# Attention and mixture of experts on one core: the first batch's loads, the last groups' banks and evictions, the count, and the order of the instructions

## Chip, core and metric

One core of one Trainium2 chip runs the whole program. The metric is the device time of one execution in microseconds (us). The core has a matrix engine, PE (its weight loads are listed as PEld), a vector engine, DVE, a scalar engine, ACT, a general one, POOL, and SP, which here only issues DMAs. Each has its own instruction stream and runs it in order; they wait for each other by semaphores.

## The reference

`x` has 4 batches of 11456 tokens with 128 channels; `inducing` has 32 rows.

```python
def mab(q, kv):
    s = scale * (q @ kv.transpose(0, 2, 1))
    s = s - s.max(-1, keepdims=True)
    a = np.exp(s)
    a /= a.sum(-1, keepdims=True) + 1e-09
    return a @ kv
h = mab(I, x)          # 32 rows for each batch, over all its tokens
y = mab(x, h)          # each token over the 32 rows
```

Each row of `y` then goes through the best of 8 experts: `logits = y @ w_gate`, `e = argmax`, weight `p` = the softmax's value there, output `p * (relu(y @ w1[e]) @ w2[e])` with 1024 hidden units. All of it is float32.

## The kernel before

**Tiling.** A batch is cut into 6 groups of 15 x 128 tokens. A group is loaded by column (`xt`, 960 KB: channels on the partitions, used for scores), and for the sums over tokens also by row (`xn`, 967.5 KB). For some groups (`TURNED`) the rows are not loaded: PE transposes the column tile (L315) and ACT or DVE copies it (L325, L327). There are 12 buffers for `xt`, 3 for `xn`, 3 for results (`ob`), 8 for the tokens' weights (`et`). Of the eight PSUM banks three are for scores (`fe`), one for logits (`lp`) and four for all else (`ps`). In the first batch the row tiles that are loaded go into the `ob` buffers, which nothing else uses yet.

**A batch's first half, `attend`.** Two groups at a time: scores with the inducing rows (L199, `it_s`), their peak (DVE L364), spread of the peak over the partitions (POOL L367, PE L376, DVE L382), exponent (ACT L386), 32x32 transposes (DVE L394), sums over the tokens (PE L403, collected by DVE in `hs`). After six groups `induced` forms `h`: L457 and L458 on PE, division and `hT` on DVE (L468 to L470), then the expert that fits the batch, whose weights are gathered by POOL (`w1r`, `w2r`, L510). From these PE makes a 32x128 matrix `h4` (L539, L569, L583), by which the tokens' weights give the result directly, and a bound (`thr`, L603) that says for which tokens this holds.

**A batch's second half, `tokens`.** Three groups at a time (a trio): scores with `hc` (L199), peak (DVE L646 to L650), weights (ACT L654, `et`), logits (PE L658, all three groups summed into the one `lp` bank). Then the gating of the trio on DVE and ACT (L668 to L708, factors in `c_all`). For each group: the factors are turned (DVE L715, `cb`), weights times factors (POOL L718), four expert matmuls into four `ps` banks (PE L722, K = 32 each), four evictions by ACT (L733) into `ob`, and a store issued by ACT (L736).

**At the end** the tokens not covered by the bound are counted (L786 to L795: three steps on DVE, a matmul on PE, a cast), every engine loads the count (`nleft`, L797) and branches on it (L798); if it is above zero, a slow loop treats the rest. With these inputs it is zero.

**What sets the order.** `Plan.add` takes for each step its engine, a cost, what it comes after, a rank, and the buffers or banks that it takes and gives back. `Plan.order` is a list scheduler: it places next the step that can start first by these costs, and of equal ones the one of lower rank. Loads are steps of an engine called DMA there, 2.5 us each. The kernel's instructions are written in the resulting order; the layer that records them then puts each engine's instructions in an order of its own, which may set instructions of one step apart or move them past each other. On SP's queue the loads keep the plan's order, and a load whose buffer is not free holds up those behind it.

Of the kernel before, what the change touches and what calls it, by code (L numbers as in the profile page):

```python
# [31 lines left out]
F32 = mybir.dt.float32  # L32
I32 = mybir.dt.int32
AF = mybir.ActivationFunctionType
ALU = mybir.AluOpType
# [4 lines left out]
P = 128  # L40
# [95 lines left out]
def attn_moe_kernel(ctx, tc, xT, xn, indT, wg, w1, w2, consts, out):  # L136
# [18 lines left out]
    nc.vector.memset(gz[:, 0:1], 1.0)  # L155
    hT_all = const.tile([P, B, P], F32, name="hT_all")
    c_all = const.tile([P, B, NBLK], F32, name="c_all")
    it_s = const.tile([P, M], F32, name="it_s")
    nc.vector.tensor_scalar_mul(it_s, it_sb, SCALE)

# [111 lines left out]
    def buf(op, i=0):  # L272
        k, n = op["got"][i]
        return T[k][n]
# [22 lines left out]
    def by_row(b, g, rank, load, w):  # L297


        s = S[b]  # L300
        if g not in TURNED.get(b, ()):

            def load_xn():
                w.xn = rows(buf(op))
                nc.sync.dma_start(w.xn, xn[b, :, g * GB : (g + 1) * GB, :])


            op = plan.add("DMA", 2.5, load_xn, rank=rank - 2.7, take=("ob" if b == 0 else "xn",), lag=2.0)
            return [op], (op, 0)
        turns, kept = {}, []  # L310

        def turn(k0, n):
            ps = buf(turns[k0])
            for k in range(n):
                nc.tensor.transpose(  # L315
                    ps[:, k * P : (k + 1) * P], s.xt[g][:, k0 + k].rearrange("p q t -> p (q t)"), ident
                )

        def keep(k0, n, eng):
            if k0 == 0:  # L320
                w.xn = rows(buf(turns[0], 1))
            src = buf(turns[k0])[:, : n * P].rearrange("p (k c) -> p k c", c=P)
            dst = w.xn[:, k0 : k0 + n, 0:P]
            if eng == "ACT":
                nc.scalar.copy(dst, src)  # L325
            else:
                nc.vector.tensor_copy(dst, src)  # L327
# [17 lines left out]
        return kept, (turns[0], 1)  # L345

    def pair1(b, g0, rank, begin):
# [5 lines left out]
        def load_xt(w, g):  # L353
            if begin and g == 0:
                begin()
            nc.sync.dma_start(buf(w.load), xT[b, g])
            s.xt[g] = buf(w.load)
# [90 lines left out]
    def induced(b, rank):  # L448
# [54 lines left out]
                out=w.ii, in0=w.r1, scalar=-128.0, in1=pcol, op0=ALU.mult, op1=ALU.add  # L503
            )

        def gather():
            w.w1r = pl.wraw.tile([P, F], F32, name="w1r")
            w.w2r = pl.wraw.tile([P, F], F32, name="w2r")
            for dst, src in ((w.w1r, w1), (w.w2r, w2)):
                nc.gpsimd.indirect_dma_start(  # L510
                    out=dst, out_offset=None, in_=src, in_offset=bass.IndirectOffsetOnAxis(ap=w.ii[:, :1], axis=0)
                )

        def gate_matrix():

# [110 lines left out]
        f4 = plan.add("PE", 0.9, mm_h4, [f3], r, ("ps",), ((i5, 0),), lag=0.1)  # L626
# [8 lines left out]
    def tokens(b, g0):  # L635
# [91 lines left out]
                    stop=True,  # L727
                )

        def evict(w, q):  # L730
            if q == 0:
                w.ob = buf(w.ev)[:, : NQ * GW].rearrange("p (q n) -> p q n", q=NQ)
            nc.scalar.copy(w.ob[:, q, :], buf(w.b9, q)[:, :GW])  # L733

        def store(w, g):
            nc.scalar.dma_start(out[b, g], w.ob.rearrange("p q n -> p (q n)"))  # L736

        last = None
        for u, w in enumerate(some):
# [17 lines left out]
        for u, w in enumerate(some):  # L757
            g = g0 + u
            r = NG * b + g
            w.b7 = plan.add("DVE", 0.68, lambda w=w, u=u: turn_factors(w, u), [g2], r, ("cb",))  # L760
            b8 = plan.add("POOL", 1.2, lambda w=w: weigh(w), [w.b7], r, give=((w.b7, 0),))
            w.b9 = plan.add(
                "PE", 1.1, lambda w=w: experts(w), [b8, s.h4_op], r, ("ps",) * 4, ((w.b4, 0),), lag=0.1
            )
            ev = []
            for q in range(NQ):
                take = () if ev else ("ob",)
                ev.append(
                    plan.add(
                        "ACT", 0.5, lambda w=w, q=q: evict(w, q), [w.b9] + ev[:1], r, take, ((w.b9, q),)  # L770
                    )
                )
            w.ev = ev[0]
            st = plan.add("ACT", 0.05, lambda w=w, g=g: store(w, g), ev, r)
            s.experts_op = w.b9
            plan.add("DMA", 2.8, lambda: None, [st], r - 3, give=((w.ev, 0),), lag=2.0)
# [9 lines left out]
    nc.vector.memset(c_all[64:128, :, NBLK - 1 : NBLK], 1.0)  # L786
    left = const.tile([P, B * NBLK], F32, name="left")
    nc.vector.tensor_single_scalar(left, c_all.rearrange("p b n -> p (b n)"), 0.0, op=ALU.is_gt)
    nc.vector.tensor_scalar(left, left, -1.0, 1.0, op0=ALU.mult, op1=ALU.add)
    cnt = const.tile([P, 1], F32, name="cnt")  # L790
    nc.vector.tensor_reduce(cnt, left, AX.X, ALU.add)
    psn = T["ps"][0]
    nc.tensor.matmul(psn[:, 0:1], lhsT=ones, rhs=cnt, start=True, stop=True)
    nleft = const.tile([P, 1], I32, name="nleft")
    nc.vector.tensor_copy(nleft, psn[:, 0:1])  # L795
    main.close()
    nl = nc.values_load(nleft[0:1, 0:1], min_val=0, max_val=P * B * NBLK)  # L797
    with tc.If(nl > 0):  # L798
# [191 lines left out]
```

## Time and profile before

| | |
|---|---|
| three runs | 231.03, 234.84 (median), 235.23 us |
| the profiled execution | 233.27 us, its span 231.5 us |
| PE, DVE, ACT, POOL busy | 188.5, 132.0, 104.7, 40.3 us |
| mean granted PE clock | 0.892 |
| DMA | 63.78 MB, 276 GB/s on average |

The span runs from the first to the last instruction of the one profiled execution; the rest of its time lies around it. In rows of instructions stand the start, the duration, the engine, the source line, the operation, the tile written and the tiles read, their shape, and how many instructions the row joins; in brackets the idle time before and what ended it. A fp32 matmul leaves two records. Rows of stages give the busy us and the number of records of PE, PEld, DVE, ACT and POOL, then the granted clock (1.00 is full), the share of the DMA engines' time and GB/s. Rows of waits give the total, how often, and the longest.

### The profile page before, as it was taken

The page shows a single profiled execution, that of the slowest core. Times are in us where ns is not written, and L with a number is a line of the kernel's source. Part 1 is how long each engine was busy: PE and PEld are TensorE (multiplying, and loading weights), DVE is VectorE, ACT ScalarE, POOL GpSimd, SP SyncE. Part 2 cuts the span into 40 slices and gives each one's busy share as a digit, 9 for nine tenths or more (in the row PEclk, how much of TensorE's full clock was granted, in tenths as well). Part 3 has the DMA queues.
Part 4 walks back from the last instruction along what each step waited for, and adds up shares of the span by engine and source line. Part 5 has one row for each costly group of instructions (what it writes and reads, how often), then busy time and mean ns, then how long its engine had stood idle before and what let it go on. Part 6 is the DMA issues. An engine that isn't in the chain of part 4 may idle for free.

```text
span 231.5 us, 4416 instructions
## 1 busy us (share of the span) xinstructions
PE 188.5 (81%) x1694; PEld 94.7 (41%) x1695; DVE 132.0 (57%) x400; ACT 104.7 (45%) x212; POOL 40.3 (17%) x58
## 2 busy tenths in 40 slices
PE   0897588898997799989999959999598959984840
PEld 0565364456665233544352236535122224422520
DVE  0275536674489266874894680848844998037300
ACT  2243204263350827385735841396236532845630
POOL 2000003000003500060045000410530062303200
PEclk9999889999999889999999997999959995578555
DMA  6999999995369847997999990034427524627591
GB/s 222 426 428 423 427 423 422 415 417 194 94 253 342 352 171 288 355 365 266 326 426 418 428 369 15 4 150 195 170 71 280 235 105 173 254 100 327 243 394 58
DMA packets 10252, 63.78 MB, mean 276 GB/s; under 512 B 1392, under 2 KB 1520, under 8 KB 10224
## 3 DMA queue, kind: packets, MB, share of 16 engines
q1 hardware_dynamic: 5328, 35.62, 39.2%
q10 hardware_dynamic: 3744, 23.62, 25.0%
q0 software_dynamic: 1152, 4.19, 4.8%
q8 instruction: 15, 0.25, 0.4%
q14 instruction: 13, 0.11, 0.1%
HBM read 39.83 MB, written 23.59 MB: 274 GB/s over the span
## 4 chain that ended last, share of the span: by engine, by line
PE 55%; DVE 19%; DMA 10%; ACT 6%; issue 3%; POOL 3%; SPq 0%; ACTq 0%; DVEq 0%; POOLq 0%
PE ps L722 16%; PE fe L199 15%; PE lp L658 8%; PE ps L403 8%; DMA xt<-in_xT 6%; PE ps L315 4%; DMA w1r<-in_w,ii 4%; ACT ob L733 3%; DVE cb L715 3%; POOL et L718 3%; DVE e L394 2%; DVE mx L364 2%; ACT e1t L386 2%; DVE mx L646 1%; ACT xn L325 1%
## 5 line engine op out<-in xcount | busy, mean ns | idle before, releaser
L733 ACT COPY ob<-ps 128x480 f32<-128x480 f32 x96 | 47.5, 573 | 34.0 <-PE ps L722 33.8
L722 PE MATMUL ps<-et,h 32*128 32x480 f32 x192 | 47.9, 739 | 10.3 <-POOL et L718 6.2
L718 POOL TENSOR_TENSOR et<-et,cb 128x480 f32<-128x480 f32 x24 | 28.4, 1211 | 56.2 <-DVE cb L715 36.8
L199 PE MATMUL fe<-xt,it_s 128*32 128x480 f32 x192 | 29.6, 609 | 9.7 <-DMA xt<-in_xT 9.7
L325 ACT COPY xn<-ps 128x512 f32<-128x512 f32 (+1 forms) x42 | 22.4, 570 | 26.1 <-PE ps L315 23.8
L364 DVE TENSOR_REDUCE mx<-fe 128x1 f32<-128x480 f32 x24 | 15.6, 652 | 27.9 <-PE fe L199 25.7
L722 PEld LDWEIGHTS ps<-et,h 32*128 32x128 f32 x192 | 17.6, 216 | 33.7 <-POOL et L718 13.8
L199 PE MATMUL fe<-xt,hc 128*32 128x480 f32 x192 | 29.4, 613 | 1.6 <-ACT e1t L386 1.1
L315 PE MATMUL ps<-csb,xt 128*128 128x128 f32 x180 | 27.1, 291 | 1.5 <-DMA xt<-in_xT 1.5
L658 PE MATMUL lp<-et,gzw 128*128 128x480 f32 x48 | 27.5, 661 | 0.5 <-ACT et L654 0.5
L654 ACT ACTIVATE et<-fe,rn 128x480 f32<-128x480 f32 x24 | 16.0, 671 | 26.1 <-DVE rn L650 16.6
L403 PE MATMUL ps<-xn,e 128*32 128x129 f32 x630 | 25.7, 282 | 1.7 <-DVE e L394 1.7
L315 PEld LDWEIGHTS ps<-csb,xt 128*128 128x128 f32 x180 | 21.7, 153 | 13.1 <-issue 6.2
L403 PEld LDWEIGHTS ps<-xn,e 128*32 128x32 f32 x630 | 21.8, 113 | 9.0 <-DVE e L394 2.5
L394 DVE STREAM_TRANSPOSE e<-e1t 128x480 f32<-128x480 f32 x24 | 15.1, 656 | 7.9 <-ACT e1t L386 7.8
L386 ACT ACTIVATE e1t<-fe,rn 128x480 f32<-128x480 f32 x24 | 14.8, 667 | 10.2 <-DVE rn L382 9.8
L646 DVE TENSOR_REDUCE mx<-fe 128x1 f32<-128x480 f32 x24 | 15.4, 643 | 6.1 <-PE fe L199 5.8
L715 DVE STREAM_TRANSPOSE cb<-c_all 128x480 f32<-128x480 f32 x24 | 15.4, 663 | 5.5 <-POOL et L718 5.0
L367 POOL TENSOR_TENSOR mq<-mx,csb 128x8 f32<-128x8 f32 x12 | 2.4, 201 | 91.3 <-DVE mx L364 91.2
L658 PEld LDWEIGHTS lp<-et,gzw 128*128 128x128 f32 x48 | 8.0, 207 | 13.5 <-issue 7.0
L668 DVE STREAM_TRANSPOSE lv<-lp 128x480 f32<-128x480 f32 x8 | 5.4, 671 | 14.3 <-PE lp L658 14.3
L199 PEld LDWEIGHTS fe<-xt,it_s 128*32 128x32 f32 x192 | 6.3, 113 | 16.0 <-issue 10.4
(94 smaller groups left out, 149.2 us busy)
## 6 DMA issues: line engine op xcount, KB each, us to landing
xt<-in_xT SPq DMA_DIRECT2D x24, 960.0 KB, 9.7
out<-ob ACTq DMA_DIRECT2D x24, 960.0 KB, 3.8
xn<-in_xn SPq DMA_DIRECT2D x9, 967.5 KB, 8.0
ob<-in_xn SPq DMA_DIRECT2D x3, 967.5 KB, 15.7
csb<-in_consts SPq DMA_DIRECT2D x1, 134.5 KB
w1r<-in_w,ii POOLq DMA_INDIRECT x4, 7.7
w2r<-in_w,ii POOLq DMA_INDIRECT x4, 9.3
it_sb<-in_indT ACTq DMA_DIRECT2D x1, 16.0 KB
```

The lines of the kernel that those rows point to most:

```text
L199: nc.tensor.matmul(blk(ps[32 * q : 32 * q + 32, :GW]), lhsT=lhsT, rhs=xt_g[:, :, q, :], start=True, stop=True)
L315: nc.tensor.transpose(ps[:, k * P : (k + 1) * P], s.xt[g][:, k0 + k].rearrange("p q t -> p (q t)"), ident)
L325: nc.scalar.copy(dst, src)
L364: nc.vector.tensor_reduce(s.mx[:, g : g + 1], w.ps[:, :GW], AX.X, ALU.max)
L386: nc.scalar.activation(w.et, w.ps[:, :GW], AF.Exp, bias=pr.rn)
L394: nc.vector.transpose(w.e1, w.et)
L403: nc.tensor.matmul(hp[32 * j : 32 * j + 32, :], lhsT=blk(w.e1)[:, k, :], rhs=w.xn[:, k, :], start=(n < 4), stop=(n >= 2 * GB - 4),)
L658: nc.tensor.matmul(buf(some[0].b5)[:, :GW], lhsT=s.gzw[:, u * P : (u + 1) * P], rhs=w.et, start=(u == 0), stop=(u == NW - 1),)
L715: nc.vector.transpose(blk(w.cb), c.unsqueeze(2).to_broadcast([P, GB, 32]))
L718: nc.gpsimd.tensor_tensor(out=w.et, in0=w.et, in1=w.cb, op=ALU.mult)
L722: nc.tensor.matmul(buf(w.b9, q)[:, :GW], lhsT=s.h4[32 * q : 32 * q + 32, :], rhs=w.et[32 * q : 32 * q + 32, :], start=True, stop=True,)
L733: nc.scalar.copy(w.ob[:, q, :], buf(w.b9, q)[:, :GW])
```

## The change

1. **First batch.** The column loads of batch 0 get rank r - 60 (before: r - 3), its row loads rank - 30 (before: rank - 2.7). So all six column tiles are loaded first, then the three row tiles.
2. **Last groups.** In the last trio of the last batch the middle group takes the three `fe` banks and the `lp` bank in place of the `ps` banks, and of each group's four banks DVE evicts the second and fourth. All stores of the last batch are issued by SP, in two halves of 480 KB each.
3. **Count.** It becomes three steps of the plan, after the factors of all groups; on PE it has a low rank. One DVE instruction is saved.
4. **Gather.** The two gathers become two steps of the plan with 1.1 and 1.0 us; the instructions are the same.
5. **Order.** After the plan's order has been written out, every instruction gets a dependence without a semaphore on the one before it on its engine, so the recording layer keeps the plan's order.

```diff
-            op = plan.add("DMA", 2.5, load_xn, rank=rank - 2.7, take=("ob" if b == 0 else "xn",), lag=2.0)
+            op = plan.add(
+                "DMA", 2.5, load_xn, rank=rank - 2.7 if b else rank - 30, take=("xn" if b else "ob",), lag=2.0
+            )
...
-            w.load = plan.add("DMA", 2.5, lambda w=w, g=g: load_xt(w, g), rank=r - 3, take=("xt",), lag=2.0)
+            w.load = plan.add(
+                "DMA", 2.5, lambda w=w, g=g: load_xt(w, g), rank=r - 3 if b else r - 60, take=("xt",), lag=2.0
+            )
...
-        i5 = plan.add("POOL", 2.0, gather, [i4], r, ("wraw",), lag=8.5)
+        i5 = plan.add("POOL", 1.1, lambda: gather("w1r", w1), [i4], r, ("wraw",), lag=7.9)
+        i6 = plan.add("POOL", 1.0, lambda: gather("w2r", w2), [i4], r + 0.001, lag=9.3)
...
-            nc.scalar.copy(w.ob[:, q, :], buf(w.b9, q)[:, :GW])
+            if eng == "ACT":
+                nc.scalar.copy(w.ob[:, q, :], buf(w.b9, q)[:, :GW])
+            else:
+                nc.vector.tensor_copy(w.ob[:, q, :], buf(w.b9, q)[:, :GW])
...
+            if b < B - 1:
+                nc.scalar.dma_start(out[b, g], w.ob.rearrange("p q n -> p (q n)"))
+            else:
+                h = NQ * GW // 2
+                nc.sync.dma_start(
+                    out[b, g][:, half * h : half * h + h], w.ob[:, 2 * half : 2 * half + 2].rearrange("p q n -> p (q n)")
+                )
...
+            end = b == B - 1 and g0 + NW == NG
+            banks = ("fe", "fe", "fe", "lp") if end and u == 1 else ("ps",) * 4
+            w.b9 = plan.add("PE", 1.1, lambda w=w: experts(w), [b8, s.h4_op], r, banks, ((w.b4, 0),), lag=0.1)
...
+                eng = "DVE" if end and q % 2 else "ACT"
...
+    co = plan.add("DVE", 1.2, count, [o for s in S for o in s.g2], NG * B)
+    mc = plan.add("PE", 0.5, mm_count, [co], NG * B - 9, ("ps",), lag=0.1)
+    plan.add("DVE", 0.2, copy_count, [mc], NG * B - 9, give=((mc, 0),))
+
     for op in plan.order():
         op["fn"]()
...
+    order = mybir.DependencyInfo(mybir.DependencyClass.NoSync, mybir.DependencyReason.DATA)
+    latest = {}
+    for ins in list(nc.cur_bb.bb.instructions):
+        if ins.engine in latest:
+            tc.add_manual_dep(ins, latest[ins.engine], order, reason="the plan's order")
+        latest[ins.engine] = ins.name
```

Where the instructions stand now is shown at three places. The numbers behind tile names are those of buffers; they are shifted between the two programs, since three tiles were added, and L numbers shift as well (L199 is now L202, L457 L465, L658 L666, L722 L730).

SP's queue at the start of the program, before (`xt_91` to `xt_96` are the column tiles of batch 0, `ob_106` to `ob_108` its row tiles, `xt_97` and `xn_103` the first group of batch 1):

```order
L356 DMA xt_91<-in_xT 128x1920
L356 DMA xt_92<-in_xT 128x1920
L356 DMA xt_93<-in_xT 128x1920
L356 DMA xt_94<-in_xT 128x1920
L305 DMA ob_106<-in_xn 128x1935
L356 DMA xt_95<-in_xT 128x1920
L305 DMA ob_107<-in_xn 128x1935
L356 DMA xt_96<-in_xT 128x1920
L305 DMA ob_108<-in_xn 128x1935
L356 DMA xt_97<-in_xT 128x1920
```

And now (`xt_94` to `xt_99`, `ob_109` to `ob_111`, `xt_100`):

```order
L361 DMA xt_94<-in_xT 128x1920
L361 DMA xt_95<-in_xT 128x1920
L361 DMA xt_96<-in_xT 128x1920
L361 DMA xt_97<-in_xT 128x1920
L361 DMA xt_98<-in_xT 128x1920
L361 DMA xt_99<-in_xT 128x1920
L308 DMA ob_109<-in_xn 128x1935
L308 DMA ob_110<-in_xn 128x1935
L308 DMA ob_111<-in_xn 128x1935
L361 DMA xt_100<-in_xT 128x1920
```

The column tiles of groups 4 and 5 have moved from places 6 and 8 to places 5 and 6; the last row tile stays at place 9.

PE where the last batch's `h` is formed, before (`et_119` and `et_120` are groups 0 and 1 of the batch before):

```order
L457 MATMUL ps_132<-csb,hs 128x128
L458 MATMUL ps_132<-csb,hs 128x32
L658 MATMUL lp_130<-et_115,gzw_135 128x480
L199 MATMUL fe_128<-xt_96,hc 32x480 x4
L722 MATMUL ps_134<-et_119,h_1446 128x480
L481 MATMUL ps_131<-wg_sb,hT_all 128x8
L722 MATMUL ps_133<-et_119,h_1446 128x480
L482 MATMUL ps_131<-wg_sb,hb 128x8
L722 MATMUL ps_132<-et_119,h_1446 128x480
L199 MATMUL fe_127<-xt_97,hc 32x480 x4
L199 MATMUL fe_129<-xt_98,hc 32x480 x4
L722 MATMUL ps_131<-et_119,h_1446 128x480
```

And now (`et_122` is that group 0; `xt_100` and `xt_101` are groups 0 and 1 of the last batch):

```order
L465 MATMUL ps_136<-csb,hs 128x128
L466 MATMUL ps_136<-csb,hs 128x32
L489 MATMUL ps_137<-wg_sb,hT_all 128x8
L490 MATMUL ps_137<-wg_sb,hb 128x8
L202 MATMUL fe_131<-xt_100,hc 32x480 x4
L202 MATMUL fe_132<-xt_101,hc 32x480 x4
L730 MATMUL ps_135<-et_122,h_1367 128x480
L730 MATMUL ps_134<-et_122,h_1367 128x480
L730 MATMUL ps_136<-et_122,h_1367 128x480
L730 MATMUL ps_137<-et_122,h_1367 128x480
```

The four matmuls of a group's experts stand together now, behind the small matmuls of `h` and the first scores of the last batch, and no longer with other work between them.

PE at the last logits, before (`et_116` is the last group of the third batch, `et_117` to `et_122` are groups 0 to 5 of the last one):

```order
L722 MATMUL ps_131<-et_116,h_1446 128x480
L658 MATMUL lp_130<-et_120,gzw_136 128x480
L722 MATMUL ps_134<-et_117,h_1872 128x480
L722 MATMUL ps_133<-et_117,h_1872 128x480
L722 MATMUL ps_132<-et_117,h_1872 128x480
L722 MATMUL ps_131<-et_117,h_1872 128x480
L658 MATMUL lp_130<-et_121,gzw_136 128x480
L658 MATMUL lp_130<-et_122,gzw_136 128x480
L722 MATMUL ps_134<-et_118,h_1872 128x480
L722 MATMUL ps_133<-et_118,h_1872 128x480
```

And now (`et_118` and `et_119` are groups 4 and 5 of the third batch, `et_120` to `et_125` the last batch):

```order
L666 MATMUL lp_133<-et_124,gzw_139 128x480
L730 MATMUL ps_135<-et_118,h_1367 128x480
L730 MATMUL ps_134<-et_118,h_1367 128x480
L730 MATMUL ps_136<-et_118,h_1367 128x480
L730 MATMUL ps_137<-et_118,h_1367 128x480
L666 MATMUL lp_133<-et_125,gzw_139 128x480
L730 MATMUL ps_135<-et_119,h_1367 128x480
L730 MATMUL ps_134<-et_119,h_1367 128x480
L730 MATMUL ps_136<-et_119,h_1367 128x480
L730 MATMUL ps_137<-et_119,h_1367 128x480
```

The last group's logits now come ahead of the third batch's last experts; before they came behind the experts of the last batch's first group. After these rows PE has the experts of the last batch in the order 0, 1, 4 (in `fe` and `lp`), the count's matmul, 2, 3, 5.

More of the change, by code (lines that the diff above doesn't have):

```diff
@@ L157, in attn_moe_kernel @@
     c_all = const.tile([P, B, NBLK], F32, name="c_all")
+    left = const.tile([P, B * NBLK], F32, name="left")
+    cnt = const.tile([P, 1], F32, name="cnt")
+    nleft = const.tile([P, 1], I32, name="nleft")
     it_s = const.tile([P, M], F32, name="it_s")
@@ L504, in pick, with gather @@
             )
[L506 to L512, printed above, removed]
+        def gather(n, src):
+            t = pl.wraw.tile([P, F], F32, name=n)
+            setattr(w, n, t)
+            nc.gpsimd.indirect_dma_start(
+                out=t, out_offset=None, in_=src, in_offset=bass.IndirectOffsetOnAxis(ap=w.ii[:, :1], axis=0)
+            )
         def gate_matrix():
@@ L625, in induced @@
         f3 = plan.add("DVE", 0.9, mask_g, [f2], r)
-        f4 = plan.add("PE", 0.9, mm_h4, [f3], r, ("ps",), ((i5, 0),), lag=0.1)
+        f4 = plan.add("PE", 0.9, mm_h4, [f3, i6], r, ("ps",), ((i5, 0),), lag=0.1)
         f4a = plan.add("ACT", 0.3, copy_h1, [f4], r, give=((f4, 0),))
@@ L728, in experts, with evict, store @@
                 )
-        def evict(w, q):
+        def evict(w, q, eng):
             if q == 0:
                 w.ob = buf(w.ev)[:, : NQ * GW].rearrange("p (q n) -> p q n", q=NQ)
-            nc.scalar.copy(w.ob[:, q, :], buf(w.b9, q)[:, :GW])
-        def store(w, g):
-            nc.scalar.dma_start(out[b, g], w.ob.rearrange("p q n -> p (q n)"))
+            if eng == "ACT":
+                nc.scalar.copy(w.ob[:, q, :], buf(w.b9, q)[:, :GW])
+            else:
+                nc.vector.tensor_copy(w.ob[:, q, :], buf(w.b9, q)[:, :GW])
+        def store(w, g, half):
+            if b < B - 1:
[4 more added lines that the diff above has]
+                    out[b, g][:, half * h : half * h + h], w.ob[:, 2 * half : 2 * half + 2].rearrange("p q n -> p (q n)")
+                )
         last = None
@@ L761, in tokens @@
             b8 = plan.add("POOL", 1.2, lambda w=w: weigh(w), [w.b7], r, give=((w.b7, 0),))
-            w.b9 = plan.add(
-                "PE", 1.1, lambda w=w: experts(w), [b8, s.h4_op], r, ("ps",) * 4, ((w.b4, 0),), lag=0.1
-            )
+            end = b == B - 1 and g0 + NW == NG
+            banks = ("fe", "fe", "fe", "lp") if end and u == 1 else ("ps",) * 4
+            w.b9 = plan.add("PE", 1.1, lambda w=w: experts(w), [b8, s.h4_op], r, banks, ((w.b4, 0),), lag=0.1)
             ev = []
@@ L767, in tokens @@
                 take = () if ev else ("ob",)
+                eng = "DVE" if end and q % 2 else "ACT"
                 ev.append(
                     plan.add(
-                        "ACT", 0.5, lambda w=w, q=q: evict(w, q), [w.b9] + ev[:1], r, take, ((w.b9, q),)
+                        eng,
+                        0.5 if eng == "ACT" else 0.65,
+                        lambda w=w, q=q, e=eng: evict(w, q, e),
+                        [w.b9] + ev[:1],
+                        r,
+                        take,
+                        ((w.b9, q),),
                     )
@@ L773, in tokens, with count, mm_count, copy_count @@
             w.ev = ev[0]
-            st = plan.add("ACT", 0.05, lambda w=w, g=g: store(w, g), ev, r)
             s.experts_op = w.b9
-            plan.add("DMA", 2.8, lambda: None, [st], r - 3, give=((w.ev, 0),), lag=2.0)
+            if b < B - 1:
+                st = [plan.add("ACT", 0.05, lambda w=w, g=g: store(w, g, 0), ev, r)]
+            else:
+                st = [
+                    plan.add("SP", 0.05, lambda w=w, g=g, h=h: store(w, g, h), [ev[0]] + ev[2 * h : 2 * h + 2], r)
+                    for h in range(2)
+                ]
+            plan.add("DMA", 2.8, lambda: None, st, r - 3, give=((w.ev, 0),), lag=2.0)
+        s.g2 = g2, w.b7
+    def count():
+        nc.vector.memset(c_all[64:128, :, NBLK - 1 : NBLK], 1.0)
+        nc.vector.tensor_scalar(
+            left, c_all.rearrange("p b n -> p (b n)"), 0.0, 1.0, op0=ALU.is_gt, op1=ALU.is_lt
+        )
+        nc.vector.tensor_reduce(cnt, left, AX.X, ALU.add)
+    def mm_count():
+        nc.tensor.matmul(buf(mc)[:, 0:1], lhsT=ones, rhs=cnt, start=True, stop=True)
+    def copy_count():
+        nc.vector.tensor_copy(nleft, buf(mc)[:, 0:1])
     for b in range(B):
@@ L781, in attn_moe_kernel @@
             tokens(b, g)
+    co = plan.add("DVE", 1.2, count, [o for s in S for o in s.g2], NG * B)
+    mc = plan.add("PE", 0.5, mm_count, [co], NG * B - 9, ("ps",), lag=0.1)
+    plan.add("DVE", 0.2, copy_count, [mc], NG * B - 9, give=((mc, 0),))
     for op in plan.order():
         op["fn"]()
[L786 to L795, printed above, removed]
+    order = mybir.DependencyInfo(mybir.DependencyClass.NoSync, mybir.DependencyReason.DATA)
[4 more added lines that the diff above has]
+        latest[ins.engine] = ins.name
     main.close()
```

## The prediction

> **What bounds the kernel now.** I read busy time, granted clock (PEclk, 1.00 is full) and DMA share by stage. I cut the span where PE forms the `h` of a batch (L457), because a batch's tokens cannot begin before its `h`.
>
> ```profile
> span 231.5 us, 4416 instructions
> core 0: us, PE busy (x) PEld busy (x) DVE busy (x) ACT busy (x) POOL busy (x), PEclk, DMA share, GB/s
> 0.00:32.40 32.40, 21.84 (x288) 14.96 (x289) 13.08 (x29) 8.62 (x16) 1.92 (x14) 0.95 0.95 389
> 32.40:62.80 30.40, 25.92 (x345) 16.48 (x343) 18.32 (x55) 11.36 (x24) 2.76 (x6) 1.00 0.80 316
> 62.80:113.00 50.20, 46.08 (x444) 22.47 (x445) 33.24 (x105) 27.20 (x56) 9.88 (x13) 0.97 0.80 299
> 113.00:161.00 48.00, 43.10 (x416) 21.27 (x417) 31.42 (x100) 26.64 (x55) 9.50 (x11) 0.96 0.65 263
> 161.00:223.00 62.00, 51.23 (x206) 19.23 (x205) 35.78 (x113) 30.86 (x64) 16.25 (x14) 0.75 0.50 202
> ```
>
> Up to 32.4 us the DMAs are full (0.95) and PE is not. In the middle PE leads, at 85 to 92% of each stage, at full clock. The last stage is the odd one: half the matmul records of the stages before it (206 against 444 and 416) and yet the longest, 62 us, at a clock of 0.75; ACT and DVE are busy for only about half of it. So it is bound by waits in turn. The table of waits for 161 us to the end names them:
>
> ```profile
> POOL et L718 <- DVE cb L715: 32.3, 3, 13.3
> ACT ob L733 <- PE ps L722: 23.2, 11, 3.9
> DVE lv L668 <- PE lp L658: 11.7, 2, 9.1
> ```
>
> In turn: PE brings the logits late to DVE, DVE the factors late to POOL, POOL the weights late to PE, PE the results late to ACT. The prices are therefore looked for at the two ends, the first `h` and the stage after the last one.
>
> **Start.** A load of 960 KB moves at some 428 GB/s here, thus one every 2.3 us.
>
> ```profile
> xt<-in_xT SPq DMA_DIRECT2D x24, 960.0 KB, 9.7
> 10.00:15.00 5.00, 5.00 (x41) 3.11 (x39) 3.36 (x7) 2.49 (x5) 0.20 (x1) 1.00 1.02 430
> 6.45 1.83 PE L199 MATMUL fe<-xt,it_s 128*32 128x480 f32 x8 [6.45 <-DMA xt<-in_xT]
> 25.20 0.67 DVE mx L364
> 28.34 3.20 PE L403 MATMUL ps<-ob,e 128*32 128x129 f32 x58 [1.74 <-DVE e L394]
> 32.38 0.49 PE L457 MATMUL ps<-csb,hs 128*128 128x128 f32 x2
> ```
>
> The first group is there at 6.45. The column load of group 5 was the eighth of the queue, so 6.45 + 7 x 2.3 = 22.6; its peak is taken at 25.2, its sums start 3.1 us later and end at 31.5, and `h` follows at 32.4. Now it is the sixth: 18.0. The last row load stays ninth, 6.45 + 8 x 2.3 = 24.9, and with the column chain out of the way this becomes the bound: 24.9, about 2 us for the sums of groups 4 and 5, then the scores of the next batch's first group, which stand ahead of `h` in PE's order and whose load is tenth (27.2 + 0.9): `h` at 28.3, **4.1 us** earlier. The bytes are the same and batch 1's loads land as before, so batch 1 can give some of it back: bounds 0 and -4.1. I take -3, since the second stage is bound by DMA only for its first half (share 0.80) and PE then has batch 0's tokens earlier.
>
> **Order.** In the old order three groups of experts are split: other matmuls stand between their four banks. In the new one all 24 stand whole.
>
> ```profile
> 92.13 1.07 PE L722 MATMUL ps<-et,h 32*128 32x480 f32 x2
> 206.29 1.09 PE L722 MATMUL ps<-et,h 32*128 32x480 f32 x8
> 165.84 1.07 PE L722 MATMUL ps<-et,h 32*128 32x480 f32 x2 [2.53 <-POOL et L718]
> 167.16 1.47 PE L722 MATMUL ps<-et,h 32*128 32x480 f32 x2
> 169.09 1.96 PE L722 MATMUL ps<-et,h 32*128 32x480 f32 x2
> 166.94 0.56 ACT L733 COPY ob<-ps 128x480 f32<-128x480 f32 x1 [3.93 <-PE ps L722]
> 175.51 0.56 ACT L733 COPY ob<-ps 128x480 f32<-128x480 f32 x1 [3.87 <-PE ps L722]
> 176.54 1.95 ACT L733 COPY ob<-ps 128x480 f32<-128x480 f32 x4
> ```
>
> One bank alone (two records) takes 1.07, four together 1.09. The split group near 90 us (three pieces) thus costs 2 x 1.07 = 2.1 us of PE: **-2** (0 to -2.1). The one at 166 us is dear: its four evictions last from 166.94 to 176.07, 9.1 us where a whole group takes 1.95, and the next groups queue behind them for the same banks. 7.2 us at most; **-5**, since DVE and POOL go on meanwhile and the order of `h` differs (0 to -7.2).
>
> By the last `h` the new order has done two logits and one score group more than the old. That work moves from the last stage ahead of it: nothing in the sum.
>
> The last logits are the next place:
>
> ```profile
> 203.78 2.58 PE L658 MATMUL lp<-et,gzw 128*128 128x480 f32 x4
> 206.40 0.68 DVE L668 STREAM_TRANSPOSE lv<-lp 128x480 f32<-128x480 f32 x1 [9.11 <-PE lp L658]
> 212.19 3.61 POOL L718 TENSOR_TENSOR et<-et,cb 128x480 f32<-128x480 f32 x3 [13.30 <-DVE cb L715]
> 216.15 5.93 PE L722 MATMUL ps<-et,h 32*128 32x480 f32 x16 [0.72 <-ACT ob L733]
> 218.11 0.56 ACT L733 COPY ob<-ps 128x480 f32<-128x480 f32 x1 [0.73 <-PE ps L722]
> 220.79 0.56 ACT L733 COPY ob<-ps 128x480 f32<-128x480 f32 x1 [0.73 <-PE ps L722]
> ```
>
> They are done at 206.4, and 5.8 us of gating lie between them and the first weighting. Now they stand two expert groups earlier, ahead of the third batch's last one. Such a group takes 1.95 us where ACT sets the pace and 2.7 at this clock (evictions of two groups begin at 218.11 and 220.79, each after 0.73 idle). Two make 3.9 to 5.4: **-4** (0, if ACT is still behind, to -5.4).
>
> **Last groups and end.** The last three took from the first weighting, 212.19, to the last eviction, 220.79 + 1.95 = 222.74: 10.5 us. DVE's copy of a PSUM bank is bounded by its 128x512 row, 0.69 against ACT's 0.56, so two banks on each cost 1.4 us a group instead of 1.95. But in PE's order the last batch now ends 0, 1, 4, count, 2, 3, 5. Group 4 has banks of its own; it also has to wait for its weighting, second of the last three, and group 2, long ready, stands behind it, with four evictions on ACT. From the first weighting: 2 x 1.2 until group 4 is weighted, 1.1 and 1.1 for groups 4 and 2 on PE, 1.95 to evict group 2, 0.7 for the first bank of group 3, 3 x 1.4 to evict 3, 4 and 5: 11.5 us at full clock, +1; some 2 us more at half clock. I take **+1.5** (-2, if group 2 comes through in time, to +3).
>
> ```profile
> out<-ob ACTq DMA_DIRECT2D x24, 960.0 KB, 3.8
> 10.21 0.69 DVE L327 COPY xn<-ps 128x512 f32<-128x512 f32 x1 [1.22 <-PE ps L315]
> 222.79 0.58 PE L793 MATMUL ps<-cnt,ones 128*128 128x1 f32 x2 [0.71 <-ACT ob L733]
> 223.41 0.16 DVE L795 CAST nleft<-ps 128x1 int32<-128x1 f32 x1 [6.84 <-PE ps L793]
> L797 PEldq TENSOR_LOAD <-nleft x1: 1124/1124/1124, 223.6 to 223.6; - x1
> L798 PEldq COMPARE_BRANCH x1: 5113/5113/5113, 224.8 to 224.8; - x1
> ```
>
> After the last matmul (216.15 + 5.93 = 222.1) come an eviction, the count on PE and DVE, the load of `nleft` (1.1), PE's branch (5.1) and 1.6 us of closing, until 231.5: 9.4 us. With the count done before, load, branch and closing remain, 7.8: **-1.6**. PE's branch covers the last store (3.8 us to landing); without that cover the two half-stores would cost their issue, 2 x 0.3. The added stores of the last batch stand on SP behind its last load, where nobody waits; the load of `nleft` on SP, ahead of group 2's store, holds back only stores. On DVE the count stands between the last factors and the first eviction, where the 2.4 us of weighting cover it. The gathers keep their two instructions.
>
> **Sum** against the profiled execution, 233.27 us (span 231.5): -3 - 2 - 5 - 4 + 1.5 - 1.6 = -14.1, thus **219 us**. The median of the three runs, 234.84, lies 1.6 above that execution, so this is 6 to 7% faster. Each term at its better end gives 211; each at its worse end, without the end's gain, 236; not all fall on one side: 212 to 226 for this case.
>
> **The clock.** PE's busy time is full from 195 to 205 us, and yet the clock is half:
>
> ```profile
> 195.00:200.00 5.00, 5.00 (x15) 2.41 (x13) 1.47 (x3) 3.73 (x8) 3.51 (x3) 0.50 0.24 102
> 200.00:205.00 5.00, 5.00 (x13) 1.74 (x13) 0.00 (x0) 2.90 (x7) 0.00 (x0) 0.50 0.71 295
> ```
>
> By these rows a PE that only waits for banks does not hold its clock; the last stage loses some 0.25 x 62 = 15 us of PE to it. [...]
>
> **Rivals.** (1) Hidden anyway: batch 1's loads set the pace to 54 us and swallow the start; ACT and POOL wait elsewhere in the last stage, which keeps 2 us of its 9. 233.3 - 2 - 2 - 1.6 = 228 us. For it: DMA share 0.80 in the second stage, and a tail whose waits pass from engine to engine. Against it: those waits have one origin each, and the order removes it. (2) The last stage runs at full clock: whole groups and no late logits take away the gaps, and half of the 15 us goes as well: 219 - 7.5 = 211.5. For it: the clock is 1.00 in the second stage, where PE's matmuls follow each other closely. (3) The new order gains nothing: places like group 2 behind group 4 cost what the others bring; 233. A late load speaks for it:
>
> ```profile
> 131.02 0.33 SPq L356 DMA_DIRECT2D xt<-in_xT  x1
> 139.35 0.99 PE L199 MATMUL fe<-xt,it_s 128*32 128x480 f32 x2 [3.28 <-DMA xt<-in_xT]
> ```
>
> 8.3 us from issue to use; the new order again has only about 5 us of PE work between the scores that free this buffer and those that need it, so this stall stays. (4) Slower: with a fixed order PE cannot fill its waits with other matmuls, the gaps drop the clock in the middle too, and each us at half clock loses 0.5. It decides from 41 us on (219 + 20.5 = 239.5); with 45 of the 130 us between 32 and 161 at half clock, 242. Against it: that stretch stands at 0.96 to 1.00, and the order moves little there.
>
> **Chances.** My forecast 0.60, (1) 0.18, (2) 0.10, (3) 0.06, (4) 0.06. A measurement of this kernel tells about 2% from no change, thus 230 and 239.5. Faster: the forecast, (2) and two thirds of (1), 0.82; the same: the rest of (1) and (3), 0.12; slower: (4), 0.06. The range reaches from rival (2)'s better half to just beyond (1): 208 to 231.
>
> **What would show it.** Right: first `h` (then L465) near 28 us; the last between 155 and 160; no idle of 9 us before DVE's last L676; evictions of the first expert group after the last `h` within 2 us or so; `nleft` read by PE right after its last matmul. Wrong: the `h` of batch 1 still at 62 or later (start swallowed); 55 us or more from the last `h` to the last matmul; a clock under 0.9 between 32 and 161 us; PE waiting over 4 us for group 4 while group 2's weights are done.

## The result, and the profile after

The changed kernel takes 219.14 us (median of 4 runs, 217.24 to 219.62), the one before 234.81 (231.03 to 235.23): a ratio of 0.939 with an interval of 0.932 to 0.945. The forecast of 219.0 us holds. The profiled execution after took 217.24 us (span 215.5), 16.0 less than that of before. Runs over 1.5% above the fastest of the same kernel count as slow and are left out of the times below; of the kernel without ties two of four remain.

Busy time by stage of the changed kernel, cut at the same places (first `h` matmul of each batch, now L465; last expert matmul):

```profile
core 0: us, PE busy (x) PEld busy (x) DVE busy (x) ACT busy (x) POOL busy (x), PEclk, DMA share, GB/s
0.00:29.40 29.40, 20.79 (x287) 13.45 (x288) 12.79 (x29) 8.62 (x16) 1.93 (x14) 1.00 0.95 385
29.40:63.10 33.70, 30.23 (x371) 17.12 (x367) 24.62 (x74) 12.90 (x27) 3.09 (x8) 0.95 0.89 355
63.10:105.60 42.50, 38.53 (x407) 20.92 (x407) 26.43 (x80) 25.80 (x53) 9.40 (x11) 1.00 0.88 314
105.60:160.20 54.60, 47.07 (x443) 21.84 (x439) 42.04 (x124) 27.57 (x56) 13.27 (x15) 0.94 0.57 226
160.20:206.50 46.30, 39.71 (x194) 16.63 (x194) 33.94 (x100) 27.24 (x56) 12.66 (x11) 0.81 0.68 268
```

The stages took 32.4, 30.4, 50.0, 48.1 and 61.1 us before (first `h` matmuls at 32.4, 62.8, 112.8 and 160.9, last expert matmul over at 222.1). So the first `h` is 3.0 us earlier, the second is not earlier at all, the third is 7.2 earlier, the fourth 0.7, and the last stage is 14.8 us shorter. These boundaries also move work (the new order does more of the tokens' work before the last `h`), so a stage alone doesn't name a cause.

The waits of the last stage, from 160 us to the end:

```profile
ACT ob L742 <- PE ps L730: 15.6, 11, 6.4
POOL et L726 <- DVE cb L723: 15.2, 2, 13.9
PEld fe L730 <- POOL et L726: 4.1, 1, 4.1
...
DVE lv L676 <- PE lp L666: 1.8, 1, 1.8
```

POOL's and ACT's totals (32.3 and 23.2 before) have shrunk by half and by a third; DVE's wait for the logits, 11.7 before, is 1.8. (The long wait of POOL before its weighting, 13.3 us, is still there: 13.9.) PE at the last `h`, the last logits and the last groups:

```profile
160.22 0.49 PE L465 MATMUL ps<-csb,hs 128*128 128x128 f32 x2
162.58 0.36 PE L489 MATMUL ps<-wg_sb,hT_all 128*128 128x8 f32 x2 [1.73 <-ACT ex L698]
164.92 1.09 PE L730 MATMUL ps<-et,h 32*128 32x480 f32 x8
...
183.52 1.07 PE L666 MATMUL lp<-et,gzw 128*128 128x480 f32 x2
...
195.42 1.18 PE L730 MATMUL fe<-et,h 32*128 32x480 f32 x3 [2.62 <-POOL et L726]
```

ACT's first eviction after it:

```profile
166.03 1.95 ACT L742 COPY ob<-ps 128x480 f32<-128x480 f32 x4 [3.55 <-PE ps L730]
```

The group that took 9.1 us to evict now takes 1.95; the last logits are done at 184.6 in place of 206.4; and PE waits 2.6 us for the weighting of group 4.

### The profile page after: what moved, and what is told of

Read it like the earlier page. It is cut to its first block, busy times and chain, and to the rows that moved or that the text cites. A ratio compares the mean times of both kernels' runs of the same rounds, so it can differ in the third digit from the quotient of the medians.

```text
span 215.5 us, 4442 instructions
## 1 busy us (share of the span) xinstructions
PE 176.4 (82%) x1694; PEld 90.0 (42%) x1695; DVE 140.6 (65%) x405; ACT 102.3 (47%) x206; POOL 40.4 (19%) x58
## 4 chain that ended last, share of the span: by engine, by line
PE 33%; DVE 30%; DMA 24%; ACT 4%; issue 4%; POOL 1%; SPq 1%; ACTq 0%; DVEq 0%; POOLq 0%
DMA xt<-in_xT 19%; PE fe L202 9%; PE ps L730 9%; PE lp L666 7%; DMA w1r<-in_w,ii 5%; DVE cb L723 4%; DVE ls L687 2%; DVE lv L676 2%; PE ps L320 2%; ACT ob L742 2%; DVE mx L654 2%; PE ps L408 2%; DVE mx L369 2%; ACT et L662 2%; DVE rs L684 1%
## 5 line engine op out<-in xcount | busy, mean ns | idle before, releaser
L742 ACT COPY ob<-ps 128x480 f32<-128x480 f32 x88 | 43.0, 573 | 24.6 <-PE ps L730 24.5
L730 PE MATMUL ps<-et,h 32*128 32x480 f32 x184 | 41.1, 695 | 1.6 <-ACT ob L742 1.3
L330 ACT COPY xn<-ps 128x512 f32<-128x512 f32 (+1 forms) x42 | 22.4, 568 | 35.5 <-PE ps L320 35.1
L202 PE MATMUL fe<-xt,it_s 128*32 128x480 f32 x192 | 25.5, 602 | 10.2 <-DMA xt<-in_xT 8.9
L666 PE MATMUL lp<-et,gzw 128*128 128x480 f32 x48 | 26.4, 635 | 3.6 <-ACT et L662 3.1
L320 PEld LDWEIGHTS ps<-csb,xt 128*128 128x128 f32 x180 | 21.7, 152 | 14.8 <-issue 8.0
L369 DVE TENSOR_REDUCE mx<-fe 128x1 f32<-128x480 f32 x24 | 15.2, 646 | 18.6 <-PE fe L202 18.6
L202 PE MATMUL fe<-xt,hc 128*32 128x480 f32 x192 | 25.2, 611 | 1.4 <-ACT e1t L391 1.2
L730 PEld LDWEIGHTS ps<-et,h 32*128 32x128 f32 x184 | 18.1, 204 | 19.7 <-issue 10.5
L662 ACT ACTIVATE et<-fe,rn 128x480 f32<-128x480 f32 x24 | 15.6, 665 | 14.1 <-DVE rn L658 12.3
L408 PE MATMUL ps<-xn,e 128*32 128x129 f32 x630 | 22.3, 274 | 0.0
L408 PEld LDWEIGHTS ps<-xn,e 128*32 128x32 f32 x630 | 18.9, 110 | 7.8 <-issue 3.0
L654 DVE TENSOR_REDUCE mx<-fe 128x1 f32<-128x480 f32 x24 | 15.3, 638 | 1.2 <-PE fe L202 1.0
L666 PEld LDWEIGHTS lp<-et,gzw 128*128 128x128 f32 x48 | 7.4, 193 | 15.6 <-ACT et L662 10.1
L202 PEld LDWEIGHTS fe<-xt,it_s 128*32 128x32 f32 x192 | 4.7, 111 | 17.3 <-issue 9.4
L676 DVE STREAM_TRANSPOSE lv<-lp 128x480 f32<-128x480 f32 x8 | 5.4, 672 | 7.7 <-PE lp L666 7.7
## 6 DMA issues: line engine op xcount, KB each, us to landing
ob<-in_xn SPq DMA_DIRECT2D x3, 967.5 KB, 17.4
```

What stands on the lines that cost most here:

```text
L202: nc.tensor.matmul(blk(ps[32 * q : 32 * q + 32, :GW]), lhsT=lhsT, rhs=xt_g[:, :, q, :], start=True, stop=True)
L320: nc.tensor.transpose(ps[:, k * P : (k + 1) * P], s.xt[g][:, k0 + k].rearrange("p q t -> p (q t)"), ident)
L369: nc.vector.tensor_reduce(s.mx[:, g : g + 1], w.ps[:, :GW], AX.X, ALU.max)
L408: nc.tensor.matmul(hp[32 * j : 32 * j + 32, :], lhsT=blk(w.e1)[:, k, :], rhs=w.xn[:, k, :], start=(n < 4), stop=(n >= 2 * GB - 4),)
L654: nc.vector.tensor_reduce(m, w.ps[:, :GW], AX.X, ALU.max)
L662: nc.scalar.activation(w.et, w.ps[:, :GW], AF.Exp, bias=w.rn)
```

## The experiments

Theory A, the forecast's own: the gain is in the order, above all in expert groups that are no longer cut in pieces on PE. Rival B: it comes from the last groups' banks, evictions and stores. Rival C: from the loads at the start. Theories A2, D and H came up on the way and are said where they are tested.

Times are medians, ratios are to the kernel before on the same chip. That kernel's own median lay between 233.5 and 235.5 us from one set of runs to the next, so a difference between kernels of different sets is known to some 2 us. Differences are given by the medians and by the ratios where the two do not agree.

### Without the ties; old loads; old last groups

Three kernels undo one part of the change each. Part 5 (the loop that ties each instruction to the one before it on its engine) is left out; the nine loads of batch 0 get the old order in the written-out plan, all else stays:

```
+    ops = plan.order()
+    at = [i for i, op in enumerate(ops) if op["engine"] == "DMA"][:9]
+    for i, o in zip(at, [ops[at[k]] for k in (0, 1, 2, 3, 6, 4, 7, 5, 8)]):
+        ops[i] = o
...
```

and the last groups are as before (`ps` banks, ACT evicts, whole stores).

> The changed kernel without its ties (part 5): the recording layer sets each engine's order again. The last logits keep their early place; groups 0 and 4 of the last batch and group 4 of the third are split between their banks again. Theory A (the gain of the last stage, 61.1 to 46.3 us, comes from the order): the split groups cost about what the forecast gave them, 4 to 8 us, so 223 to 227 us, with waits of ACT for PE's experts of several us back after the last h. Theory B (it comes from the last groups' banks, evictions and half-stores): all of that is kept, so 217 to 220 us. Theory C (it comes from the loads at the start): kept too, 217 to 220 us.

> The changed kernel with the order of batch 0's nine loads as before (column tiles of groups 4 and 5 at places 6 and 8) and every other instruction in the changed kernel's order. Forecast's term and theory C: 3 us slower, 221 to 223 us. What the traces suggest (the second h is at 63.13 us against 62.80, so the 3 us of the first h were swallowed): first h 3 to 4 us later, second h at 63 again, 218.5 to 219.7 us, no difference that 3 rounds tell.

> The changed kernel without part 2: the last trio's middle group takes the ps banks and stands in its place (2, 3, 4, 5), ACT evicts all, ACT issues whole stores. Theory A and the forecast's term (the last groups cost 1.5 us, since group 2 stands behind group 4): 1.5 us faster, 216.5 to 219 us. Theory B: the last groups' banks and evictions are worth most of the last stage's gain, so 225 to 230 us; if they are only worth what two engines instead of one save in evictions, 3 x 0.55, about 221.

**Measured.** Without the ties 234.97 and 237.79 us: no faster than the kernel before, and 16 to 19 us over the changed one, where theory A had 4 to 8 and the others none. Theories B and C fall as accounts of the whole gain. With the old loads 222.93 us, ratio 0.957 (0.942 to 0.972), inside the 221 to 223 that the forecast's term gave; with the old last groups 216.8 us, ratio 0.931 (0.913 to 0.949), not told apart from the changed kernel's 0.939.

For the loads the two traces show more than the medians. The first `h` is 3.8 us later than in the changed kernel, the second 1.0, the last expert matmul 5.4. What grows on the way is time at half clock, 36.7 us up to that matmul (mean clock over the span 0.897) against 28.0 (0.914):

```profile
21.60:25.00 3.40, 0.98 (x16) 0.52 (x20) 1.36 (x3) 0.32 (x2) 0.00 (x0) 1.00 1.03 431
25.00:28.40 3.40, 3.40 (x64) 3.02 (x53) 0.66 (x1) 0.00 (x0) 0.20 (x1) 0.50 1.01 424
69.40:72.80 3.40, 1.99 (x8) 0.53 (x4) 2.56 (x8) 1.70 (x4) 2.44 (x3) 1.00 0.97 291
72.80:76.20 3.40, 3.40 (x45) 2.53 (x48) 0.00 (x0) 1.46 (x3) 0.00 (x0) 0.50 0.96 370
```

Read these rows of stages (old loads) in pairs: PE is busy for 0.98 and 1.99 of 3.4 us, and the next 3.4 us run at 0.50. The 8.7 us more at half clock are up to 4.3 us of work. So by these traces the load order brings 3.8 us at the first `h` and about 1 us at the second; the rest of the 3.8 us between the medians would then be work at half clock. One trace of each kernel does not settle that.

### The ties alone

> The kernel before with the ties alone (part 5): experts whole, the last logits at their old late place (behind the experts of the last batch's first group), old loads, old last groups, count at the end. Theory A: the split groups' part of the forecast without the logits' part, 7 us faster, 226 to 229 us; if the late logits alone hold the last stage, 232 to 235. Theories B and C: 233 to 236 us, no change.

**Measured:** 219.83 us, ratio 0.948 (0.932 to 0.963). The ties alone, on the kernel before, give what the whole change gives within what these runs can tell (0.939, 0.932 to 0.945). Here the last logits still stand at the late place that the prediction priced at 4 us. It is not theory A's 226 to 229 either: the order is worth nearly twice the 7 us that the split groups were given.

### Whose order: PE's, or that of the others

Ties on PE alone, then on the other engines alone:

```
+        if ins.engine == mybir.EngineType.PE and ins.engine in latest:
```
```
+        if ins.engine != mybir.EngineType.PE and ins.engine in latest:
```

> The kernel before with the ties on PE's instructions alone; DVE, ACT and POOL are ordered by the recording layer. PE's order is that of the fully tied kernel before (219.8 us), instruction by instruction. Theory A (what costs are the expert groups that are split on PE): the whole gain is here, 219 to 223 us. Theory D (it is the order on the other engines, DVE's above all: in the kernel before POOL's L367 waits 91.2 us in all for DVE's peaks, in the tied one 48.6): little of it is here, 229 to 235 us.

> The kernel before with the ties on DVE, ACT, POOL and SP, and none on PE, whose order is the recording layer's (groups of experts split again). Theory A: 229 to 235 us. Theory D: 219 to 224 us. If the orders of the engines only have to agree with each other, both partly tied kernels lie above 226 us.

**Measured:** 222.09 us (0.942, 0.935 to 0.949) with PE tied, 228.21 us (0.968, 0.960 to 0.977) with the others tied. PE's order carries most, as theory A said: 13.4 us in this set of runs. But the kernel with the others tied is 7.3 us faster too, which A doesn't give, and theory D's 219 to 224 is missed as well. (PE's order there is not that of the kernel before: four groups of experts are cut once each, none of them behind the last `h`. A part of the 7.3 us can be that.) So the order on PE is not the only cause. The time from the start of PE's `h` matmul (L457) to the end of `hc` on DVE (L488), in us by batch, shows the second one:

```
before          2.6   4.0   5.1   7.2
changed         2.3   2.3   2.4   2.9
all tied        2.3   3.2   2.6   2.7
PE tied         2.3   3.6   5.1   7.2
others tied     2.3   3.0   2.3   2.7
```

DVE at the last `h` in the kernel before, whose matmuls are over at 161.5:

```profile
162.92 0.44 DVE L706 RECIPROCAL se<-se 128x45 f32<-128x45 f32 x1
163.74 0.68 DVE L715 STREAM_TRANSPOSE cb<-c_all 128x480 f32<-128x480 f32 x1
164.34 0.15 DVE L468 TENSOR_SCALAR rv<-ps 128x32 f32<-128x32 f32 x1
164.42 0.66 DVE L715 STREAM_TRANSPOSE cb<-c_all 128x480 f32<-128x480 f32 x1
165.00 0.31 DVE L469 RECIPROCAL rv<-rv 128x32 f32<-128x32 f32 x1
165.82 0.68 DVE L715 STREAM_TRANSPOSE cb<-c_all 128x480 f32<-128x480 f32 x1 [0.51 <-POOL et L718]
166.42 0.25 DVE L470 TENSOR_TENSOR hT_all<-rv,ps 128x128 f32<-128x128 f32 x1
```

The same steps (now L476 to L478) in the changed kernel, where these matmuls are over at 160.9:

```profile
161.54 0.18 DVE L476 TENSOR_SCALAR rv<-ps 128x32 f32<-128x32 f32 x1
161.76 0.35 DVE L477 RECIPROCAL rv<-rv 128x32 f32<-128x32 f32 x1
162.15 0.29 DVE L478 TENSOR_TENSOR hT_all<-rv,ps 128x128 f32<-128x128 f32 x1
```

The six short steps from `h` to `hc` are 1.6 us of DVE work. In the recording layer's order the gating of an earlier trio stands ahead of them and between them, down to a factor's transpose that itself waits for POOL. With PE tied and DVE not, PE stands there:

```profile
156.28 0.36 PE L481 MATMUL ps<-wg_sb,hT_all 128*128 128x8 f32 x2 [3.51 <-DVE hT_all L470]
156.85 0.59 PE L482 MATMUL ps<-wg_sb,hb 128*128 128x8 f32 x2 [0.21 <-DVE hb L477]
```

What each order is worth can be read from the last stage, from the last `h` matmul to the last expert matmul. It holds the same work in all four kernels (205 matmul records); in this order the rows are the kernel before, all tied, PE tied, others tied:

```profile
160.95:222.08 61.13, 51.07 (x205) 19.07 (x203) 35.83 (x113) 30.26 (x63) 16.25 (x14) 0.75 0.49 198
153.35:208.46 55.11, 42.90 (x205) 16.39 (x203) 38.51 (x113) 30.35 (x63) 16.17 (x14) 0.78 0.56 225
150.41:211.35 60.94, 49.28 (x205) 18.63 (x203) 36.29 (x113) 30.32 (x63) 16.06 (x14) 0.72 0.50 199
163.26:218.25 54.99, 43.03 (x205) 16.53 (x203) 38.60 (x113) 29.43 (x61) 16.16 (x14) 0.80 0.56 225
```

Behind the last `h` no expert group is cut in the last three. With PE tied the groups are whole and `hc` is as late as before, and the stage is as long as before (60.9 and 61.1 us). Where `hc` comes early as well, it is 6 us shorter. So whole groups alone do not shorten this stage. What PE's order alone brings lies ahead of the last `h`, which comes at 150.4 us in place of 160.9. There PE's own busy time falls: from the first to the third `h` it is 71.9 us before and 65.5 with PE tied, for the same work. Only one of the three cut groups lies in that stretch, so most of this fall is not named by the cut groups of experts. All this is read from one trace of each kernel.

### What each of them costs

Theory A2 looks for the cost in cut groups of scores as well, theory H in a late `hc`. Three kernels put one suspected cost into the tied kernel before, more of it than the untied order had, and keep the ties. A cut group of scores or experts:

```
...
+        if "then" in op:
+            op["cut"][2](range(op["cut"][1]))
+            op["then"]["fn"]()
+            op["cut"][2](range(op["cut"][1], NQ))
...
```

and `divide_h`, with what hangs on it, moved behind DVE work that doesn't need it:

```
...
+        while work < late:
+            j += 1
+            op = ops[j]
+            if names & set(op["from"]):
+                held.append(op)
+                names.add(op["n"])
+            else:
+                first.append(op)
+                work += op["work"] if op["engine"] == "DVE" else 0.0
+        ops[i : j + 1] = first + held
...
```

> The tied kernel before (219.8 us) with 11 of the groups of four score matmuls against hc (L199) cut in two, one matmul ahead of the next step of PE and three behind it, as the recording layer does it five times in the kernel before. All else is in the tied order. Theory A2 (what the untied order costs is PE's own time in cut groups of four, of scores as well as of experts; whole eight records take 1.01 us, a cut pair 0.99 and 1.01): 11 x 1.0 us more PE time, and 7 to 11 us in all, so 227 to 231 us. Theory H (it is the chain behind h on DVE, held up by other work): 220 to 222 us.

> The tied kernel before with 12 groups of experts (L722) cut, three banks ahead of the next step of PE and one behind it. Theory A, as the forecast priced it (1.07 us of PE for each cut, and ACT's evictions held up besides): 12 x 1.07 = 13 us and more, 230 to 235 us. If a cut group costs its PE time only where PE has no slack: 224 to 229 us. Theory H: 220 to 222 us.

> The tied kernel before with the steps behind h on DVE (L468 to L488, and what hangs on them) moved behind other DVE work in batches 1, 2 and 3: some 1.7, 2.8 and 4.9 us of it, which is how much later hc came in the untied kernel before than the 2.3 us that it takes at best. No group is cut. Theory H: most of the 9.4 us come back, 224 to 229 us. Theories A and A2: 219 to 222 us.

**Measured.** Scores cut 11 times: 223.31 us (0.954, 0.944 to 0.964), 3.5 us by the medians and 1.5 by the ratios; A2's 227 is not reached. Experts cut 12 times: 235.9 us (1.005, 1.000 to 1.010), 16.1 or 13.3 us, just above theory A's 230 to 235. `hc` later: 230.7 us (0.985, 0.976 to 0.994), 10.9 or 8.7 us, theory H's price and a little more, because `hc` came 15.8 us later in the three batches and not the 9.4 meant. Spread evenly, an expert cut costs 1.1 to 1.35 us, a score cut 0.1 to 0.3, and a microsecond of late `hc` 0.55 to 0.7. The score cuts are not told from nothing, since the tied kernel itself is known only to some 2 us. All three kernels have the ties, and two of them lose most of the gain: it is the order that the ties keep that counts, not the ties as such.

The stage from the last `h` to the last logits in the kernel with the experts cut (columns as in the rows of stages above):

```profile
159.60:209.20 49.60, 43.40 (x169) 13.11 (x167) 30.16 (x93) 21.41 (x43) 12.54 (x11) 0.69 0.42 165
```

And in the tied kernel:

```profile
153.40:192.20 38.80, 31.55 (x169) 10.77 (x167) 29.97 (x93) 20.84 (x43) 12.57 (x11) 0.82 0.52 205
```

The same 169 matmul records, 11.9 us more PE time and a lower clock. Four of the twelve cuts lie in this stage; the four banks that stand alone take 7.0 us there, three of them at half clock by their length (1.96 us for the one at 205.3, in place of 1.07). The rest goes with the lower clock of the others (0.69 against 0.82 over the stage). The eight cuts ahead of the last `h` cost less: it comes 6.2 us later. In the kernel with the late `hc`, where the last `h` matmul starts at 156.4, PE gets to the next step of that chain only here:

```profile
168.18 0.59 PE L481 MATMUL ps<-wg_sb,hT_all 128*128 128x8 f32 x2 [1.56 <-DVE hT_all L470]
```

That is 11.8 us after `h`, where the changed kernel takes 2.4 (160.22 to 162.58).

The kernel before had 6 expert cuts (three groups in nine pieces), 5 score cuts, and `hc` 7.8 us later than the tied one in batches 1 to 3: 6.6 to 8.1, 0.5 to 1.5 and 4.3 to 5.5, together 11.4 to 15.1 us. The ties brought 12.2 (by the ratios) to 13.7 (by the medians). The sum comes out near the gain, but it proves little, because these costs do not add. With PE tied and `hc` as late as before, only 2.3 us are lost by the medians and nothing by the ratios; and PE's order alone brings 13.4 us, where its cuts are priced at 7.1 to 9.6. The last stage shows how they overlap: it takes 60.9 us with a late `hc` and whole groups, 61.1 with a late `hc` and cut groups, 66.8 with an early `hc` and four groups cut, and 55.1 with neither. By these traces either of the two holds the stage up without the other.

### Start on the tied kernel, joined gathers, whole stores

> The kernel before with the ties and with part 1, batch 0's columns loaded first. If the start is worth its 3 us (the changed kernel with the old load order took 222.9 against 219.1), then 215 to 217.5 us against 219.8 of the tied kernel before, and the other parts of the change (last groups, count, gathers) cost about 3 us together. If what that run lost is only where its half-clock windows fell, 219 to 221 us.

> The changed kernel with part 4 undone: the two gathers are one step of the plan again (2.0 us, 8.5 until they have landed). The instructions are the same, but the plan's order changes: the last logits of the last batch stand behind group 0 of that batch again, and the matmuls that need the gathered weights stand later. Theory A's term for late logits: 4 us slower, 222 to 225 us. If PE's wait for the first gather in the changed kernel (L546 at 120 us, 3 us, and a half clock for 6.8 us) is what the two steps cost: 3 us faster, 215 to 217 us.

> The changed kernel with the last batch's stores as before, whole and issued by ACT; the banks and DVE's evictions of part 2 stay, and PE and DVE keep their order. If the end of the changed kernel is SP's last half-store (issued 0.8 us after the last eviction, landed 6.4 us later): the span ends 7 us after the last matmul in place of 9.0, 217 us against 219.1. If the branch on the count still sets the end: no change, 219 us.

**Measured:** 221.2 us (0.935, 0.926 to 0.945), 220.2 us (0.939, 0.932 to 0.946) and 221.8 us (0.943, 0.927 to 0.959). None is told apart from the changed kernel. What the start adds to the tied kernel before is not settled: 1.4 us slower by the medians, 3 us faster by the ratios; in its trace the second `h` is at 63.1 us against 61.5. In the kernel with joined gathers the last logits stand two expert groups later again, and the time is the same within 1.1 us: the second test in which their place shows no worth. Whole stores do not shorten the end, although the last one is issued right behind its eviction; both expectations for it are missed. Issue and landing of the last batch's stores in the changed kernel (halves, by SP):

```profile
L751 SPq DMA_DIRECT2D out<-ob x12: 332/340/1327, 189.9 to 208.1; - x12
DMA to landing us min/median/max: 2.5/3.5/6.4
```

And of all stores where they are whole and issued by ACT:

```profile
L748 ACTq DMA_DIRECT2D out<-ob x24: 338/338/363, 73.2 to 211.5; - x24
DMA to landing us min/median/max: 3.7/3.8/8.6
```

The last half-store is issued at 208.1 and DMA is busy until 213.9; the last whole one at 211.5, and its last packet is moved at 218.6, since two groups end 1.7 us apart and their 960 KB each queue up. Both spans end right behind: the end is now set by the last store.

## Why the prediction was right, point by point

- **Sum.** Forecast -14.1 against the profiled execution, measured -16.0 there and -15.7 by the medians. Eleven of the fourteen came from the three terms of the order, and the order is the cause: the ties alone bring nearly all, and without them nothing is left. But the gain is not made up as the sum had it: terms that were wrong cancel, so that the total came out within 2 us is in part luck.
- **Split expert groups, -2 and -5.** That they cost is right, and by the price of a cut the six are 6.6 to 8.1 us. The prediction priced two of the three groups (the third is cut once, at 191.9 us). The -5 for the last stage is not borne out as it stands: with PE tied these groups are whole and the stage takes 60.9 us against 61.1; it gets shorter only where `hc` is early as well.
- **Late logits, -4.** Not borne out. The step "they stand two expert groups earlier" shows no effect in either kernel that takes it back (0.7 and 1.1 us by the medians). What the prediction missed is another cost in the same stage: the chain from `h` to `hc` on DVE. With whole groups on PE in both, the last stage is 6 us shorter where this chain runs undisturbed; by its price it is 4.3 to 5.5 us over the kernel. The kernel before's trace showed it (hc 2.6, 4.0, 5.1 and 7.2 us after `h`, with rows of the gating between its steps), but the prediction follows the new order on PE and ACT alone. That this cost is about as large as the term that failed is luck.
- **Cut scores.** Not counted; 0.5 to 1.5 us by their price, not told from nothing.
- **PE's order ahead of the last `h`.** The forecast had -2 for the group near 90 us. The ties alone bring the last `h` from 160.9 to 153.4 us, with PE alone tied to 150.4. Which of PE's steps make up the rest is open.
- **Start, -3 for the first `h`'s 4.1.** The first `h` came 3.0 earlier, the second, at 63.1, not at all: what the prediction named as the sign that the start is swallowed. The kernel with old loads gives 3.8 us back, most of it half clock by the traces, and on the tied kernel the medians and the ratios differ on the sign. The traces leave about 1 us of the start at the second `h`, as rival 1 had it for this place; whether the whole kernel keeps 0 or the 3 us is not settled.
- **Last groups, +1.5.** Not told from zero (216.8 us without part 2). PE does wait for group 4, 2.6 us.
- **End, -1.6.** From the last matmul to the end 9.4 us became 9.0. `nleft` is read by PE early, at 204.6 us (223.6 before), as forecast. The step that failed is "without that cover the two half-stores would cost their issue, 2 x 0.3": they cost their landing, 5.9 us.
- **Signs.** First `h` 29.4 (near 28), last 160.2 (155 to 160), no idle of 9 us before DVE's last L676 (1.8 us is the most in the last stage), the eviction in 1.95 us: these came.
- **Rivals.** (2) the clock of the last stage rose only from 0.75 to 0.81. The last 18 us before the final matmul (188.7 to 206.5) ran at 0.50 throughout, so the last groups stayed at half clock. That PE's waits for banks take the clock down is the prediction's own reading of two rows, and rivals (2) and (4) rest on it; the runs show the half clock, not what brings it on. (3) and (4) did not come: from the first to the last `h` the clock stood at 0.94 to 1.00.

Open is why the changed kernel without ties is no better than the one before, although its last logits are early: it has six expert cuts and three score cuts, which by their prices are 7 to 9 us of its 16 or more, and at the last `h` its `hc` is as early as in the changed kernel (2.9 us). The order of group 4 and group 2 alone, and the count alone, were not tried.

## What to carry to other kernels

When the order of instructions changes, list every engine's order around each short serial chain, not only that of the busiest one: what stands between the steps of the chain delays all that hangs on it. Matmuls that take no longer together than one alone (here a group's four banks, 1.09 us against 1.07) should be kept together, and cuts counted over the whole program. Two costs that hold up the same stage do not add: test each with the other taken away. When a cover at the end is removed, look for what lands last, not for what is issued last.

## What the runs showed of the hardware

**The half clock comes in stretches.** In the changed kernel the granted clock is 0.50 from 31.7 to 35.1 us, from 117.0 to 123.9 and from 188.7 on; in the kernel before from 27.7 to 31.2, 78.9 to 82.4, 140.4 to 143.8, 167.7 to 174.5, 191.6 to 205.2 and from 212.1 on. The stretches that end within the span last 3.4, 6.8 or 13.7 us. With the old loads two begin at 25.0 and 72.8 us, in the rows above. What brings them on these traces do not show, and PE's busy share alone does not decide it: ahead of the one at 72.8 PE is busy for 1.99 of 3.4 us (59%); in the changed kernel it is busy for the same 1.99 us from 69.3 to 72.7, and the next 3.4 us run at 1.00.

**DVE's busy time depends on its order.** The tied orders take some 6 us more of DVE than the untied ones for the same instructions, here the page of the kernel with PE alone tied:

```profile
PE 177.8 (81%) x1694; PEld 89.2 (40%) x1695; DVE 132.2 (60%) x400; ACT 104.8 (47%) x212; POOL 40.1 (18%) x58
```

And with the others tied:

```profile
PE 184.8 (81%) x1694; PEld 93.9 (41%) x1695; DVE 138.7 (61%) x400; ACT 105.9 (47%) x212; POOL 40.2 (18%) x58
```

In the untied order the next row often starts before the one ahead of it has ended (164.34 + 0.15 and 164.42 above), where the steps alternate between two chains; in the tied order each step of a chain starts behind the one that it needs (161.54 + 0.18 and 161.76). The durations of DVE's rows add up to 149.4 us in the kernel before, where DVE is busy for 132.0, and to 152.7 in the changed one, where it is busy for 140.6 with five instructions more: 17.4 and 12.1 us of overlap. The longest steps are no slower (652 ns for a peak at L364, 646 at L369 now). By these two traces most of the 6 us is overlap that is gone, not slower instructions. They did not cost the kernel its gain.
